# Batch 0's opening rearranged: compact transposes, f32 warm-ups, a later read of the state, and first loads on two queues

## The chip, the cores and the metric

The kernel runs on one core of one Trainium2 chip. The metric is device time in microseconds (us), as a median of executions. The profile is one execution taken by the hardware profiler; its span is some 1.8 us shorter than the timed value (147.9 against 149.7 us). In its lines PE is TensorE, PEld its weight loads, DVE is VectorE, ACT is ScalarE, POOL is GpSimd, SPq and ACTq are the instruction queues of SyncE and ScalarE where they issue transfers, and L85 is a line of the kernel's source.

## The reference

Attention between tokens and a small recurrent state, in both directions, and then a layer of two experts with an elementwise maximum:

```python
# x (8, 8, 512, 64), state (8, 8, 32, 64), f32
a  = softmax(scale * x @ state.T);  xread = a @ state      # 512 rows per batch
a2 = softmax(scale * state @ x.T);  sread = a2 @ x         # 32 rows per batch: "the state's read"
X  = concatenate([xread, sread], axis=2)                   # as 4352 rows of 512
out = maximum(X @ w1, X @ w2) @ w_out                      # 512 -> 1024 -> 512
```

The kernel uses maximum(h1, h2) = h2 + relu(h1 - h2). So it needs W1 - W2 for the first layer, and adds W2 @ W_out, which it computes once, to the second. It also multiplies the small state into W1 - W2 first, so that each token needs only its row of `a` and the product.

## The kernel before

All loads go through SyncE's queue. The first ones, in order: batch 0's state (64 KB, in pieces of 256 B), batch 0's x in two halves of 512 KB (even and odd heads, in pieces of 1 KB), then W2 and W_out (pieces of 2 KB), W1, and batch 1's x.

```python
def load_x(b, parts=1):
    xf_t[b] = xio.tile([128, H, NC * D], F32, ...)
    for g in range(parts):
        nc.sync.dma_start(out=xf_t[b][:, g::parts, :], in_=x[b, g::parts].rearrange("h (p c) d -> p h (c d)", c=NC))

def load_states(bs):
    nc.sync.dma_start(out=s_f[...], in_=state[bs].rearrange("b (q h) n d -> (h n) (b q) d", q=2))
...
load_states(first)
load_x(0, 2)
for ch in range(2):
    load_w(w2f, moe_w2, ch); load_wo(2 * ch); load_wo(2 * ch + 1)
load_w(w1f, moe_w1, 0, 2)          # first half of W1, in two pieces
load_w(w1f, moe_w1, 1)
load_x(1)
```

The work up to the first matmul on W1, in program order (each engine runs its own part in this order). `warm_up(n)` issues n matmuls on zeros that are meant to keep the array at its full rate; the letters A, V, P name ScalarE, VectorE, GpSimd.

```python
warm_up(6)
cast_states("V", first)
states(first)                  # two transposes of the state
warm_up(9)
cast_x(0, (("A", even heads), ("V", even), ("P", odd), ("V", odd)))  # f32 -> bf16, with a ones column
u_xt(0, 0, "V")                # transposes of the even half of x: 16 of 128x64
warm_up(2)
u_xt(0, 1, "A")                # the odd half
u_exp(0, 0); warm_up(2); u_exp(0, 1); warm_up(3)      # scores, exp
w_cast(w2b, w2f, 0, "PA")
u_norm(0, 0, nc.vector)        # row sums "es", reciprocals "er", multiply: a = e * er
u_norm(0, 1, nc.vector)
w_t(0, 0, "A"); w_t(0, 1, "A") # transposes of W2
u_sr(0)                        # the state's read: 32 matmuls
wo_cast(0, "P"); wo_cast(1, "P"); warm_up(1)
...w_wo(0, i)                  # W2 @ W_out, first quarter of the sum
u_at(0, "V")                   # transposes of a
w_cast(w2b, w2f, 1)
...w_wo(1, i)
w_t(1, 0, "V"); w_t(1, 1, "A")
negate_states()                # V: sneg = -state
wo_cast(2, "P"); wo_cast(3, "P")
u_srt(0); warm_up(2)           # one transpose of the state's read
...w_wo(2, i), casts of W1's first half on P, A, V, A, ...w_wo(3, i)
u_sw(0, 0)                     # state @ W1 - state @ W2: the first matmuls on W1
...
w_sub(0); w_sub(1)             # P: W1 - W2, first half
l1(0, {}, range(0, 4))         # layer 1 of batch 0
```

The softmax here doesn't subtract the row's maximum and nothing guards it: scores larger than these inputs give would overflow.

Of the kernel before, what the change touches and what calls it, by code (L numbers as in the profile page):

```python
# [8 lines left out]
F32 = mybir.dt.float32  # L9
BF16 = mybir.dt.bfloat16  # L10
# [5 lines left out]
def kernel(  # L16
# [42 lines left out]
    def copy(eng, o, i):  # L59
        if eng == "A":  # L60
            nc.scalar.copy(o, i)  # L61
        elif eng == "V":
            nc.vector.tensor_copy(o, i)  # L63
        else:
            nc.gpsimd.tensor_copy(o, i)  # L65
# [8 lines left out]

    xf_t = {}

    def load_x(b, parts=1):
        xf_t[b] = xio.tile([128, H, NC * D], F32, tag="xf", name="xf")
        for g in range(parts):
            nc.sync.dma_start(out=xf_t[b][:, g::parts, :], in_=x[b, g::parts].rearrange("h (p c) d -> p h (c d)", c=NC))  # L80

    s_f = stage.tile([128, 2 * B, D], F32)

    def load_states(bs):
        nc.sync.dma_start(out=s_f[:, 2 * bs.start:2 * bs.stop],  # L85
                          in_=state[bs].rearrange("b (q h) n d -> (h n) (b q) d", q=2))

    first, second, rest = slice(0, 1), slice(1, 3), slice(3, 8)
# [11 lines left out]
        nc.sync.dma_start(out=wof[:, 2 * q:2 * q + 2],  # L100
                          in_=moe_w_out.rearrange("(k p) n -> p k n", p=128)[:, 2 * q:2 * q + 2])

    load_states(first)
    load_x(0, 2)
    for ch in range(2):
        load_w(w2f, moe_w2, ch)
        load_wo(2 * ch)
# [5 lines left out]
    load_x(2)  # L113

    ident = consts.tile([128, 128], BF16)
    warm = consts.tile([128, 512], BF16)
    nc.gpsimd.memset(warm, 0.0)  # L117
    make_identity(nc, ident)
    sbd = consts.tile([128, B, H, 2, Ns], BF16)
# [8 lines left out]
    def warm_up(n):  # L128
        p = bank()
        for k in range(n):  # L130
            nc.tensor.matmul(p, warm[:, 0:128], warm, start=(k == 0), stop=(k == n - 1))  # L131


    s_bf = stage.tile([128, 2 * B, 2, D], BF16)
# [16 lines left out]
    def states(bs):  # L151
        p = bank(BF16)
        n = bs.stop - bs.start
        for q in range(2 * n):
            nc.tensor.transpose(p[:, q * 128:(q + 1) * 128], s_bf[:, 2 * bs.start + q].rearrange("p u d -> p (u d)"), ident)
        for g in range(2):
            copy("V", sbd[64 * g:64 * g + 64, bs, :, g, :],
                 p[64 * g:64 * g + 64, 0:256 * n].rearrange("p (b h n) -> p b h n", b=n, h=H))
# [16 lines left out]
    def cast_x(b, parts=(("P", slice(0, 8)),)):  # L175
        new_x(b)
        xp = st[b]["xp"] = xio.tile([128, H, NC, 66], BF16, tag="xp", name="xp")
        nc.gpsimd.memset(xp[:, :, :, 64:65], 1.0)
        for e, hs in parts:
            copy(e, xp[:, hs, :, 0:64], xf_t[b][:, hs].rearrange("p h (c d) -> p h c d", c=NC))  # L180

    def compact_x(b, g, eng="A"):
        new_x(b)
        if g == 0:
            st[b]["xc"] = at.tile([128, H, NC * D], BF16, tag="xc", name="xc")
        copy(eng, st[b]["xc"][:, 4 * g:4 * g + 4], xf_t[b][:, 4 * g:4 * g + 4])


    def d_xt(b):
# [2 lines left out]
    def u_xt(b, g, eng):  # L192
        d = st[b]
        p = bank(BF16)
        for i in range(4):
            for c in range(NC):
                k = 2 * i + c // 2
                nc.tensor.transpose(p[64 * (c % 2):64 * (c % 2) + 64, k * 128:(k + 1) * 128], d["xp"][:, 2 * i + g, c, 0:64], ident)
        copy(eng, d["xt"].rearrange("p (i g u) t -> p g i (u t)", g=2, u=2)[:, g], p.rearrange("p (i w) -> p i w", i=4))

    def u_sc(b, g, mul=nc.gpsimd):
# [28 lines left out]
    def u_sr(b):  # L230

        d = st[b]
        d["sr"] = at.tile([128, 2, D], BF16, tag="sr", name="sr")
        d["rr"] = at.tile([128, 2], F32, tag="rr", name="rr")
        p = bank()
        for g in range(2):
            for c in range(NC):
                for i in range(4):
                    nc.tensor.matmul(p[32 * i:32 * i + 32, g * 65:g * 65 + 65], d["e"][:, g, i, c, :],  # L239
                                     d["xp"][:, 2 * i + g, c, 0:65],  # L240
                                     start=(c == 0 and g == 0), stop=(c == NC - 1 and g == 1))
        pv = p[:, 0:130].rearrange("p (g u) -> p g u", g=2)
        nc.vector.reciprocal(d["rr"], p[:, 64:130:65])
        nc.vector.tensor_mul(d["sr"], pv[:, :, 0:64], d["rr"].unsqueeze(2).to_broadcast([128, 2, D]))
# [16 lines left out]
    def u_srt(b):  # L261
        p = bank(BF16)
        nc.tensor.transpose(p[:, 0:128], st[b]["sr"].rearrange("p g d -> p (g d)"), ident)
        copy("A", sread_t[:, :, b * Ns:(b + 1) * Ns], p[:, 0:128].rearrange("p (i n) -> p i n", i=4))
        del st[b]
# [36 lines left out]
    def l1(b, fill, fs=range(NF), engs=None):  # L302
        if fs[0] == 0:
            R[b] = big.tile([128, NF, NC * 128], BF16, tag="r", name="r")
        for f in fs:
            p = bank()
            for g in range(2):
                nc.tensor.matmul(p, SW[b][:, g, f * 128:(f + 1) * 128], AT[b][:, g, :], start=(g == 0), stop=(g == 1))  # L308
            relu(R[b][:, f, :], p, engs and engs[f - fs[0]])
            run(*fill.get(f, ()))  # L310
# [10 lines left out]
    def l2_add(b, c, fs):  # L321
        for f in fs:
            nc.tensor.matmul(OB[b][1 + c], R[b][:, f, c * 128:(c + 1) * 128], wo[:, f, :], start=False, stop=(f == NF - 1))  # L323
# [94 lines left out]
    def fillers(b):  # L418
        fill = {}

        def put(slot, *units):
            fill.setdefault(slot, []).extend(units)

        n = b + 1
        if n < B:
            put(7, lambda: u_sc(n, 0), lambda: u_sc(n, 1))
            put(8, lambda: u_sr(n))
        if n + 1 < B:
            put(8, lambda: compact_x(n + 1, 0), lambda: compact_x(n + 1, 1))
        if n < B:  # L430
            put(9, lambda: d_at(n))
            put(10, lambda: u_sw(n, 0, 1, 2))
        if n + 1 < B:
            put(10, lambda: d_xt(n + 1))
        if n < B:
            put(11, lambda: u_srt(n))
        return fill

    for b in range(B):
        SW[b] = swt[:, b % 2]  # L440
    warm_up(6)
    cast_states("V", first)
    states(first)
    warm_up(9)
    cast_x(0, (("A", slice(0, 4, 2)), ("V", slice(4, 8, 2)), ("P", slice(1, 4, 2)), ("V", slice(5, 8, 2))))
    u_xt(0, 0, "V")
    warm_up(2)
    u_xt(0, 1, "A")
    u_exp(0, 0)
    warm_up(2)  # L450
    u_exp(0, 1)
    warm_up(3)
    w_cast(w2b, w2f, 0, "PA")
    u_norm(0, 0, nc.vector)
    u_norm(0, 1, nc.vector)
    w_t(0, 0, "A")
    w_t(0, 1, "A")
    u_sr(0)
    wo_cast(0, "P")
    wo_cast(1, "P")  # L460
    warm_up(1)
    for i in range(4):
        w_wo(0, i)
    u_at(0, "V")
# [5 lines left out]
    negate_states()  # L470
    wo_cast(2, "P")
    wo_cast(3, "P")
    u_srt(0)
    warm_up(2)
    for i in range(4):
        w_wo(2, i)
    for e, i in (("P", slice(0, 1)), ("A", slice(1, 2)), ("V", slice(2, 3)), ("A", slice(3, 4))):
# [9 lines left out]
    l1(0, {}, range(0, 4))  # L487
    w_sub(2, nc.vector)
    w_sub(3, nc.vector)
    compact_x(1, 0)  # L490
    compact_x(1, 1)
    d_xt(1)
    load_states(rest)
    cast_x(1, (("A", slice(0, 4)), ("A", slice(4, 8))))
    cast_states("P", second)
    compact_x(2, 0, "P")
    compact_x(2, 1, "P")
    d_xt(2)
    load_x(3)
    for c in range(NC):  # L500
# [1 line left out]
    l2_add(0, 0, range(0, 4))  # L502
    l2_add(0, 1, range(0, 4))
    states(second)
    l2_add(0, 2, range(0, 4))
    u_sw(0, 1)
    l2_add(0, 3, range(0, 4))
    l1(0, {}, range(4, 8))
    u_sw(1, 0)
    u_exp(1, 0)  # L510
    u_exp(1, 1)
# [61 lines left out]
```

## Time and profile before

Before the change: 149.76 us (149.66 to 149.92, 4 runs). The moments, from the timelines of single engines:

| moment (us from the span's start) | before |
|---|---|
| state landed, VectorE casts it | 2.91 |
| even / odd half of x landed, cast | 5.13 / 6.67 |
| transposes of x begin, even / odd half | 6.13 / 7.62 |
| first row sums "es" | 9.84 |
| TensorE waits for W_out's third quarter, then goes on | 0.72, then 18.71 |
| W1's first half landed | 21.64 |
| first matmul on W1 | 22.25 |
| layer 1 of batch 0 | 23.92 |
| layer 1 of batch 1 | 40.01 |

A line of a timeline gives start, duration, engine, source line, operation, output and inputs, shapes and count; a bracket at its end is idle time of that engine just before, and what ended it.

### The profile page before, as it was taken

To read this page: it belongs to the slowest core of one execution; us is meant where nothing else is said; L and a number is where in the kernel's file an instruction comes from. 1 tells how busy PE (TensorE), PEld (TensorE's weight loads), DVE (VectorE), ACT (ScalarE), POOL (GpSimd) and SP (SyncE) were. 2 spreads that over 40 slices of the span, in tenths; PEclk is the share of its full clock that TensorE was granted. 3 is DMA by queue.
4 is the path that set the end of the run, shared out by engine and by line. 5 is a ranking of instruction groups with operands and counts; after the bars stand their busy time and mean duration, and the time that the engine had idled before them with its cause. 6 is when DMAs were issued, how large, how long until landed. Compare 5 with 4: busy or idle time off the path is not lost.

```text
span 147.9 us, 3003 instructions
## 1 busy us (share of the span) xinstructions
PE 139.4 (94%) x1228; PEld 67.4 (46%) x1249; DVE 81.7 (55%) x150; ACT 75.7 (51%) x127; POOL 44.2 (30%) x48
## 2 busy tenths in 40 slices
PE   6979899999999999999999999999999999999991
PEld 2445433434454345434443454454445434764460
DVE  5448728758887187545836581668067635721130
ACT  3175538577576268446834691477167036521011
POOL 3144269551967310640072037004100500000000
PEclk9999999999999999999999999999999999999999
DMA  4999999879999939793979497760556031502423
GB/s 75 379 387 387 387 385 340 269 138 231 262 230 307 303 68 297 273 195 118 285 226 178 177 280 188 139 284 2 106 111 284 0 75 58 226 0 70 141 89 131
DMA packets 37982, 29.89 MB, mean 202 GB/s; under 512 B 24912, under 2 KB 33360, under 8 KB 37072
## 3 DMA queue, kind: packets, MB, share of 16 engines
q1 hardware_dynamic: 37824, 29.56, 69.6%
q8 instruction: 10, 0.16, 0.4%
q10 hardware_dynamic: 144, 0.13, 0.3%
q14 instruction: 4, 0.03, 0.1%
HBM read 15.20 MB, written 8.91 MB: 163 GB/s over the span
## 4 chain that ended last, share of the span: by engine, by line
PE 74%; DMA 14%; SPq 7%; ACT 2%; issue 1%
PE acc L323 34%; PE ps L308 16%; DMA xf<-in_x_dram 11%; PE acc L319 8%; SPq L97 4%; DMA xt<-xc 3%; PE ps L280 3%; PE ps L216 2%; PE ps L367 2%; PE acc L377 2%; PE ps L239 2%; SPq L100 2%; PE acc L357 1%; ACT xc L61 1%; PE acc L375 1%
## 5 line engine op out<-in xcount | busy, mean ns | idle before, releaser
L323 PE MATMUL acc<-wo,r 128*128 128x512 bf16 x238 | 58.3, 379 | 0.5
L323 PEld LDWEIGHTS <-r 128*128 128x128 bf16 x248 | 23.9, 98 | 28.3 <-issue 0.2
L298 DVE TENSOR_SCALAR r<-ps 128x512 bf16<-128x512 f32 x32 | 22.1, 692 | 13.6 <-PE ps L308 13.6
L226 POOL TENSOR_TENSOR a<-e,er 128x512 bf16<-128x512 bf16 x14 | 14.4, 1049 | 50.5 <-ACT e L219 29.6
L308 PE MATMUL ps<-aT,swt 128*128 128x512 bf16 x127 | 29.1, 379 | 0.3 <-DVE swt L63 0.2
L63 DVE COPY ob<-acc 128x512 f32<-128x512 f32 (+1 forms) x17 | 11.0, 655 | 30.2 <-PE acc L323 29.8
L61 ACT COPY ob<-acc 128x512 f32<-128x512 f32 (+1 forms) x16 | 9.2, 573 | 28.9 <-PE acc L323 13.1
L296 ACT ACTIVATE r<-ps 128x512 bf16<-128x512 f32 x32 | 19.2, 600 | 5.8 <-PE ps L308 5.2
L308 PEld LDWEIGHTS <-swt 128*128 128x128 bf16 x128 | 12.0, 98 | 15.0 <-DVE swt L63 0.8
L319 PE MATMUL acc<-swt,aT 128*128 128x512 bf16 x56 | 16.7, 380 | 0.9 <-issue 0.8
L61 ACT CAST swt<-ps 128x512 bf16<-128x512 f32 x18 | 10.0, 588 | 13.0 <-PE ps L280 13.0
L65 POOL CAST xp<-xf 128x2048 bf16<-128x2048 f32 (+1 forms) x7 | 12.2, 1745 | 11.0 <-DMA xf<-in_x_dram 11.0
L61 ACT CAST xc<-xf 128x1024 bf16<-128x1024 f32 x12 | 11.9, 1051 | 1.6 <-DMA xf<-in_x_dram 1.6
L223 DVE TENSOR_REDUCE es<-e 128x16 f32<-128x512 bf16 x16 | 10.6, 660 | 3.6 <-ACT e L219 3.6
L63 DVE CAST swt<-ps 128x512 bf16<-128x512 f32 x18 | 11.6, 678 | 1.1 <-PE ps L280 1.1
L219 ACT ACTIVATE e<-ps 128x512 bf16<-128x512 f32 x16 | 8.8, 596 | 0.8
L131 PE MATMUL ps<-warm 128*128 128x512 bf16 x24 | 7.7, 444 | 1.3 <-POOL warm L117 1.3
L412 PE MATMUL acc<-wo,w2t 128*128 128x512 bf16 x30 | 7.3, 379 | 0.8 <-POOL wo L65 0.7
L319 PEld LDWEIGHTS <-aT 128*128 128x128 bf16 x62 | 4.7, 98 | 5.9 <-issue 2.5
L280 PE MATMUL ps<-wcat,sbd 64*32 64x512 bf16 x136 | 6.2, 383 | 0.1
L216 PEld LDWEIGHTS <-xt 128*128 128x128 bf16 x128 | 4.8, 98 | 2.8 <-ACT xt L61 0.8
L216 PE MATMUL ps<-sbd,xt 128*128 128x64 bf16 x128 | 5.3, 193 | 0.7 <-ACT xt L61 0.6
(74 smaller groups left out, 118.2 us busy)
## 6 DMA issues: line engine op xcount, KB each, us to landing
xf<-in_x_dram SPq DMA_DIRECT2D x7, 1024.0 KB, 7.6
out_dram<-ob SPq DMA_DIRECT2D x7, 1024.0 KB, 5.0
w2f<-in_moe_w_dram SPq DMA_DIRECT2D x2, 1024.0 KB, 8.9
wof<-in_moe_w_out_dram SPq DMA_DIRECT2D x4, 512.0 KB, 10.8
xf<-in_x_dram SPq DMA_DIRECT2D x2, 512.0 KB, 4.4
w1f<-in_moe_w_dram SPq DMA_DIRECT2D x2, 512.0 KB, 13.5
w1f<-in_moe_w_dram SPq DMA_DIRECT2D x1, 1024.0 KB, 14.4
out_dram<-ob SPq DMA_DIRECT2D x3, 256.0 KB, 2.2
```

Of the source, the lines that this page charges most:

```text
L61: nc.scalar.copy(o, i)
L63: nc.vector.tensor_copy(o, i)
L65: nc.gpsimd.tensor_copy(o, i)
L216: nc.tensor.matmul(p[:, k * 64:k * 64 + 64], d["xt"][:, 4 * i + 2 * g + cp, :], sbd[:, b, 2 * i + g].rearrange("p u n -> p (u n)"), start= ...
L223: nc.vector.tensor_reduce(d["es"][:, g], d["e"][:, g].rearrange("p i c n -> p (i c) n"), axis=mybir.AxisListType.X, op=ALU.add)
L226: mul.tensor_mul(d["a"][:, g].rearrange("p c i n -> p i c n"), d["e"][:, g], d["er"][:, g].rearrange("p (i c) -> p i c", i=4).unsqueeze(3) ...
L280: nc.tensor.matmul(pg[g][32 * i:32 * i + 32, :], sneg[gs, i, :] if k else sbd[gs, b, 2 * i + g, g, :], w[gs, i, ch * 512:(ch + 1) * 512], ...
L296: nc.scalar.activation(out=o, in_=p, func=ACTF.Relu)
L298: nc.vector.tensor_scalar(o, p, scalar1=0.0, scalar2=None, op0=ALU.max)
L308: nc.tensor.matmul(p, SW[b][:, g, f * 128:(f + 1) * 128], AT[b][:, g, :], start=(g == 0), stop=(g == 1))
L319: nc.tensor.matmul(OB[b][1 + c], AT[b][:, g, c * 128:(c + 1) * 128], SW[b][:, g, FF:WC], start=(g == 0), stop=False)
L323: nc.tensor.matmul(OB[b][1 + c], R[b][:, f, c * 128:(c + 1) * 128], wo[:, f, :], start=False, stop=(f == NF - 1))
```

## The change

Its intent is to reach W1 with fewer TensorE instructions: compact bf16 x needs 16 transposes of 128x128 instead of 32 of 128x64; 8 warm-ups in f32 replace 25 in bf16; the state's read moves behind the start of layer 1, and with it the cast with the ones column becomes one GpSimd instruction later on. Beside that, the first loads are spread over two queues.

```diff
-    def load_x(b, parts=1):
+    def load_x(b, engs=(nc.sync,)):
...
-    load_states(first)
-    load_x(0, 2)
+    load_states(first, nc.scalar)
+    load_x(0, (nc.sync, nc.scalar))
...
-    warm = consts.tile([128, 512], BF16)
+    warm = consts.tile([128, 256], F32)
...
-            for c in range(NC):
-                k = 2 * i + c // 2
-                nc.tensor.transpose(p[64 * (c % 2):64 * (c % 2) + 64, k * 128:(k + 1) * 128], d["xp"][:, 2 * i + g, c, 0:64], ident)
+            for cp in range(2):
+                k = 2 * i + cp
+                nc.tensor.transpose(p[:, k * 128:(k + 1) * 128], d["xc"][:, 2 * i + g, cp * 128:(cp + 1) * 128], ident)
...
-    warm_up(6)
+    warm_up(2)
     cast_states("V", first)
     states(first)
-    warm_up(9)
-    cast_x(0, (...))
+    warm_up(5)
+    compact_x(0, (...))             # the same four engines and parts
     u_xt(0, 0, "V")
-    warm_up(2)
     u_xt(0, 1, "A")
     u_exp(0, 0)
-    warm_up(2)
     u_exp(0, 1)
-    warm_up(3)
+    warm_up(1)
...
-    u_sr(0)
     wo_cast(0, "P")
     wo_cast(1, "P")
-    warm_up(1)
+    cast_x(0)                       # one GpSimd cast of 128x2048
...
-    u_srt(0)
-    warm_up(2)
...
     states(second)
+    u_sr(0)                         # behind layer 1's first half
...
     l1(0, {}, range(4, 8))
+    u_srt(0)
```

More of the change, by code (lines that the diff above doesn't have):

```diff
@@ L75, with load_states @@
     xf_t = {}
-    def load_x(b, parts=1):
+    def load_x(b, engs=(nc.sync,)):
         xf_t[b] = xio.tile([128, H, NC * D], F32, tag="xf", name="xf")
-        for g in range(parts):
-            nc.sync.dma_start(out=xf_t[b][:, g::parts, :], in_=x[b, g::parts].rearrange("h (p c) d -> p h (c d)", c=NC))
+        parts = len(engs)
+        for g, eng in enumerate(engs):
+            eng.dma_start(out=xf_t[b][:, g::parts, :], in_=x[b, g::parts].rearrange("h (p c) d -> p h (c d)", c=NC))
     s_f = stage.tile([128, 2 * B, D], F32)
-    def load_states(bs):
-        nc.sync.dma_start(out=s_f[:, 2 * bs.start:2 * bs.stop],
+    def load_states(bs, eng=nc.sync):
+        eng.dma_start(out=s_f[:, 2 * bs.start:2 * bs.stop],
                           in_=state[bs].rearrange("b (q h) n d -> (h n) (b q) d", q=2))
@@ L130, in warm_up @@
         for k in range(n):
-            nc.tensor.matmul(p, warm[:, 0:128], warm, start=(k == 0), stop=(k == n - 1))
+            nc.tensor.matmul(p[:, 0:256], warm[:, 0:128], warm, start=(k == 0), stop=(k == n - 1))
     s_bf = stage.tile([128, 2 * B, 2, D], BF16)
@@ L180, in cast_x, with compact_x @@
             copy(e, xp[:, hs, :, 0:64], xf_t[b][:, hs].rearrange("p h (c d) -> p h c d", c=NC))
-    def compact_x(b, g, eng="A"):
+    def compact_x(b, parts=(("A", slice(0, 4)), ("A", slice(4, 8)))):
         new_x(b)
-        if g == 0:
-            st[b]["xc"] = at.tile([128, H, NC * D], BF16, tag="xc", name="xc")
-        copy(eng, st[b]["xc"][:, 4 * g:4 * g + 4], xf_t[b][:, 4 * g:4 * g + 4])
+        xc = st[b]["xc"] = at.tile([128, H, NC * D], BF16, tag="xc", name="xc")
+        for e, hs in parts:
+            copy(e, xc[:, hs], xf_t[b][:, hs])
     def d_xt(b):
@@ L428, in fillers @@
         if n + 1 < B:
-            put(8, lambda: compact_x(n + 1, 0), lambda: compact_x(n + 1, 1))
+            put(8, lambda: compact_x(n + 1))
         if n < B:
@@ L440 @@
         SW[b] = swt[:, b % 2]
-    warm_up(6)
+    warm_up(2)
     cast_states("V", first)
     states(first)
-    warm_up(9)
-    cast_x(0, (("A", slice(0, 4, 2)), ("V", slice(4, 8, 2)), ("P", slice(1, 4, 2)), ("V", slice(5, 8, 2))))
+    warm_up(5)
+    compact_x(0, (("A", slice(0, 4, 2)), ("V", slice(4, 8, 2)), ("P", slice(1, 4, 2)), ("V", slice(5, 8, 2))))
     u_xt(0, 0, "V")
-    warm_up(2)
     u_xt(0, 1, "A")
     u_exp(0, 0)
-    warm_up(2)
     u_exp(0, 1)
-    warm_up(3)
+    warm_up(1)
     w_cast(w2b, w2f, 0, "PA")
@@ L489 @@
     w_sub(3, nc.vector)
-    compact_x(1, 0)
-    compact_x(1, 1)
+    compact_x(1)
     d_xt(1)
@@ L495 @@
     cast_states("P", second)
-    compact_x(2, 0, "P")
-    compact_x(2, 1, "P")
+    compact_x(2, (("P", slice(0, 4)), ("P", slice(4, 8))))
     d_xt(2)
```

## The prediction

> **What bounds the kernel now.** I read the page of the kernel before first, then the chain of work that ended last in order of time, then the timeline of single engines over the first 46 us, the waits, and busy time in short windows from the start.
>
> The page, its head, its row of slices and its chain by engine:
>
> ```profile
> span 147.9 us, 3003 instructions
> PE 139.4 (94%) x1228; PEld 67.4 (46%) x1249; DVE 81.7 (55%) x150; ACT 75.7 (51%) x127; POOL 44.2 (30%) x48
> ...
> DMA  4999999879999939793979497760556031502423
> GB/s 75 379 387 387 387 385 340 269 138 231 262 230 307 303 68 297 273 195 118 285 226 178 177 280 188 139 284 2 106 111 284 0 75 58 226 0 70 141 89 131
> ```
>
> TensorE is busy nearly everywhere. But the DMA engines run flat at some 385 GB/s from the second slice to the sixth, 3.7 to 22.2 us, and never again for so long. So there are two stages: up to about 22 us the loads (batch 0's x and state, W2, W_out, first half of W1) may be the limit, after it TensorE. The chain says the same: it goes through one transfer, then through matmuls alone.
>
> ```profile
> 11.39 16.16 DMA xf<-in_x_dram
> 27.55 0.02 issue
> 27.57 1.99 ACT xc L61 x2
> 29.57 0.03 ACT xp L61
> 29.59 4.50 DMA xt<-xc
> 34.10 0.04 issue
> 34.14 0.71 PE ps L216 x16
> ```
>
> The transfer is batch 1's x, queued behind all weights. The changed region ends at 22.25 us, where the first matmuls on W1 start. The timeline of TensorE before it:
>
> ```profile
> 16.44 1.06 PE L401 MATMUL ps<-ident,w2b 128*128 128x128 bf16 x16
> 17.34 0.22 PE L263 MATMUL ps<-ident,sr 128*128 128x128 bf16 x1
> 17.39 0.59 PE L131 MATMUL ps<-warm 128*128 128x512 bf16 x2
> 18.71 3.61 PE L412 MATMUL acc<-wo,w2t 128*128 128x512 bf16 x15 [0.72 <-POOL wo L65]
> 22.25 0.45 PE L280 MATMUL ps<-w1b,sbd 64*32 64x512 bf16 x8
> ```
>
> and of GpSimd, ScalarE and VectorE, the casts that it needs:
>
> ```profile
> 17.61 1.04 POOL L65 CAST wo<-wof 128x1024 bf16<-128x1024 f32 x1 [4.41 <-DMA wof<-in_moe_w_out_dram]
> 21.64 0.62 ACT L61 CAST w1b<-w1f 128x512 bf16<-128x512 f32 x1 [0.74 <-DMA w1f<-in_moe_w_dram]
> 21.64 0.43 DVE L63 CAST w1b<-w1f 128x512 bf16<-128x512 f32 x1 [2.74 <-DMA w1f<-in_moe_w_dram]
> ```
>
> The square bracket is idle time before and what ended it. TensorE was done with the work of this stage at about 17.9 us, stood 0.72 us, and went on when GpSimd had cast the third quarter of W_out, which had waited 4.41 us for its load. From 18.71 sixteen matmuls run back to back to 22.2; W1's last piece lands at 21.64 and its cast ends at 22.26. So two paths meet at 22.25, and both start at a landing. TensorE's own instruction count ahead of W1 is not what sets this moment.
>
> **What the Trainium skill says.** "DMA: Bandwidth & Descriptors", section "Issuing engines are not separate DMA queues": issuing from several engines saves only the sequencer's issue time. The trace has that time: 0.45 us for the state, 0.50 us each for two halves of x, all on one queue before W2's issue at 2.29 us. "TensorE: Matmul & The Clock Gate", Part 1: the array runs at half rate until about 3.4 us of activity and falls back after such a stretch of idleness. The trace agrees on the first: six warm-ups take 2.74 us from 1.31 us, nine later ones 2.14 us. "FP8 and Floating Point Precision", "TensorE Precision Notes": true f32 takes four passes; no f32 matmul is in this trace. "Runtime: NRT & Kernel Launch", "Instruction fetch mechanics": instructions come in blocks of 256 and crossing a block is mostly hidden. TensorE's list of waits up to 60 us holds no wait on a fetch, so I see none to save.
>
> **The change part by part.** Everything before 22.25 counts only if it moves the landings; everything after adds to TensorE's stream.
>
> 1. Transposes. 32 of 128x64 become 16 of 128x128. Sixteen old ones take 0.64 us; eight of the new shape exist already on W2 and take 0.62 us. So half the instructions save 2 x 0.02 = 0.04 us, in a stage with slack: nothing. The halves of x are cast compactly; the copy with a ones column becomes one GpSimd cast of 128x2048, 1.89 us as at 39.61. GpSimd is free from 13.2 to 17.6, so it fits with some 2.5 us to spare.
>
> 2. Warm-ups. 25 bf16 ones of 512 columns become 8 f32 ones of 256. With four passes each is worth 1024 columns, two old ones: 16 old ones' worth, 9 x 0.216 = 1.9 us less (0.216 is 1.73 us / 8 from the chain's rows of eight). This is idle filler. In instructions: 25+2+32+16+32+32+32+8+1 = 180 matmuls before W1 become 8+2+16+16+32+32+8 = 114, each with a weight load: 360 to 228.
>
> 3. State's read moved. 32 matmuls, 0.37 us (chain, 46.26), and one transpose, 0.06 us (54.09), go from the slack before 17.9 us to behind W1, into a full stream. From 22.25 to 34.10 TensorE is busy 11.35 of 11.85 us. That is 0.43 us added at the end. The transpose also takes one of four "ps" banks. At 33.61 the next pair of matmuls took the banks of the ReLUs that had ended at 33.0 and 33.54; shifted by one they wait for the one ending at 33.88, and the scores after them for that ending at 34.41. I put 0.2 us of waits on it, an estimate. Sum +0.63 us.
>
> 4. First loads. State and half of x go to ScalarE's queue, so x is issued at 0.74 instead of 1.25, and W2 at about 1.25 instead of 2.29. The windows of the start:
>
> ```profile
> 2.00:2.25 0.25, 0.25 (x2) 0.11 (x1) 0.25 (x1) 0.01 (x1) 0.00 (x0) 1.00 0.74 165
> 2.25:2.50 0.25, 0.25 (x2) 0.04 (x1) 0.25 (x1) 0.00 (x0) 0.00 (x0) 1.00 1.14 76
> 2.75:3.00 0.25, 0.25 (x3) 0.00 (x1) 0.25 (x2) 0.00 (x0) 0.00 (x0) 1.00 0.31 29
> 3.25:3.50 0.25, 0.25 (x2) 0.08 (x1) 0.00 (x0) 0.00 (x0) 0.00 (x0) 1.00 0.93 324
> ```
>
> The last column is GB/s. The state comes in near 2 us and full rate starts at 3.25, although x was issued from 1.25 on. At least the 0.51 us of issue is won; if x also stood behind the state's small pieces in the one queue, it could flow 0.7 us after its issue ends, as the state did (1.19 to about 1.9), and 1.2 us is won. I take 0.8. The bytes up to W1's first half are unchanged, and the engines are saturated to 22 us, so every later landing moves by the same: W_out's quarter 17.6 to 16.8, W1 21.64 to 20.8. TensorE must be free by then: its work before 17.9 shrinks by 0.37 + 0.06 and by three warm-ups of 0.216 in the busy stretch from 12 us on, 1.1 us in all, and its inputs come 0.8 earlier. It will be.
>
> Sum: -0.8 + 0.63 = -0.2; 149.7 - 0.2 = 149.5; as the slack could absorb some of the bank waits, I say 149.4 us.
>
> **The rivals.** (a) The transfer start does not move: state and x share sixteen engines, and the low rate from 2.25 to 3.25 is a first-access delay that any load pays. For it: the DMA share is 1.14 at 76 GB/s, so the engines were occupied and slow, not empty. Then only the added 0.4 to 0.6 us remains: 150.2. (b) TensorE becomes the limit before W1 by its clock: with the warm-ups between the stages gone it is busy perhaps 1.9 of 4 us from 6 to 10 us. If it falls to half rate, the sixteen matmuls and eight transposes from 12.5 to 16.4 take up to 3.4 us more at worst, and about 1.8 us of slack (0.72 + 1.1) take most of it: up to 151. Against it: no gap is near 3.4 us. (c) The long GpSimd cast blocks VectorE: the normalising multiply took 1.45 us beside a GpSimd cast at 10.85 and 0.69 us at 13.22. If the second one meets the 1.89 us cast, batch 0's transposes slip by about 1.5 us; the same slack takes it, so 149.4 to 150. (d) A wait on instruction fetch that no record shows ends ahead of W1: then a gain up to the 0.72 us, but the landing holds it there anyway. (e) The start moves the full 1.2 us and the moved work falls in holes: 149.7 - 1.2 + 0.2 = 148.7.
>
> **Range and chances.** Between (e) and (a) with some of (b): 148.7 to 150.5. A change over 2% is 3.0 us. Faster by that would need the 125 us after W1 to shrink, where work is only added; slower would need the half clock well beyond W1. Within 2%: 0.97; faster 0.01; slower 0.02.
>
> **What would show it.** In the changed kernel's trace: full DMA rate from about 2.4 us rather than 3.25; W1's last cast at about 20.8; first matmul on W1 at about 21.4; TensorE still standing for W_out's cast before that; u_sr's 32 matmuls and a short wait on a ReLU or a bank between 28 and 35 us; the length from the first W1 matmul to the end some 0.6 us longer than the 125.6 us of before. Wrong I am if the first W1 matmul waits for TensorE's own earlier work, if transposes or matmuls after 8 us last twice as long, or if the length after W1 changes by more than 1 us, for which I see no cause.

## The result and the profile after

The changed kernel took **153.47 us** (153.32 to 154.02, 4 runs) against 149.76 us: ratio 1.0253, 95% interval 1.0225 to 1.0281, so it is slower by 2.5%. (A ratio is the mean time of one kernel's fast runs over that of the other's fast runs of the same rounds, so it is not quite the ratio of the medians quoted.) The prediction of 149.4 us, with 148.7 to 150.5 as its range, was wrong.

The page of the kernel after, with the lines that answer to those of before:

```profile
span 151.6 us, 2977 instructions
PE 142.2 (94%) x1224; PEld 70.0 (46%) x1224; DVE 86.2 (57%) x150; ACT 75.7 (50%) x127; POOL 46.5 (31%) x49
...
DMA  4999999549969993987798397943376030602423
GB/s 110 382 378 388 387 381 333 187 82 180 212 212 312 306 193 138 307 189 133 240 311 150 64 305 260 189 152 143 68 139 274 7 69 0 281 0 58 129 95 135
```

Nothing is alarming here. The loads do start earlier: the first slice carries 110 GB/s instead of 75. Over the first 5 us, the same stretch in both, it is 180 GB/s instead of 154, so 0.13 MB more, worth some 0.34 us at 385 GB/s. The bandwidth is as good as before. What changed is who got it. Once all of x was in, hardly anything of the lead was left for the weights: the second half of W2 landed at 14.62 us instead of 14.73. The chain of work that ended last, after, in order of time (start, duration, what):

```profile
1.24 8.81 DMA xf<-in_x_dram
...
10.11 0.87 POOL xc L65
...
14.24 2.12 DVE a L227
...
18.43 1.73 PE acc L413 x8
...
21.38 1.14 DVE sneg L68
22.54 2.48 DVE sneg L68
```

Before, the chain went through the load of *batch 1's* x. Now it goes through that of half of *batch 0's* x, issued at 1.24 us and underway for 8.81 us; then through a multiply that lasts 2.12 us and two halves of the negation of the state, 3.6 us together. VectorE is on the chain for 7% of the span; before, it did not appear there. TensorE's timeline after:

```profile
9.63 1.06 PE L199 MATMUL ps<-ident,xc 128*128 128x128 bf16 x8
...
21.44 3.63 PE L413 MATMUL acc<-wo,w2t 128*128 128x512 bf16 x16 [0.34 <-DVE w2t L63]
25.00 0.93 PE L281 MATMUL ps<-w1b,sbd 64*32 64x512 bf16 x8
...
27.33 1.90 PE L309 MATMUL ps<-aT,swt 128*128 128x512 bf16 x8 [0.21 <-DVE swt L63]
```

The transposes of x begin at 9.63 instead of 6.13 us. The sixteen matmuls that before waited 0.72 us for GpSimd's cast of W_out now start at 21.44 instead of 18.71 and wait for TensorE's own earlier work (a VectorE copy of its transposes). Side by side:

| moment | before | after | later by |
|---|---|---|---|
| state cast | 2.91 | 4.72 | 1.81 |
| even / odd half of x cast | 5.13 / 6.67 | 5.00 / 10.08 | -0.13 / 3.41 |
| first row sums | 9.84 | 13.23 | 3.39 |
| W_out's third quarter multiplied | 18.71 | 21.44 | 2.73 |
| W1's first half landed | 21.64 | 20.12 | -1.52 |
| first matmul on W1 | 22.25 | 25.00 | 2.75 |
| layer 1 of batch 0 | 23.92 | 27.33 | 3.41 |
| layer 1 of batch 1 | 40.01 | 43.68 | 3.67 |
| end of the span | 147.9 | 151.6 | 3.7 |

So the 3.7 us can be followed. 3.4 us come in with x; some 0.7 us of that vanish in the slack before W_out; 0.66 us come back between the first matmul on W1 and layer 1, beside the long negation; 0.26 us come with the state's read; the rest of the kernel repeats. And W1 itself landed 1.5 us *earlier*, which helped nobody: of this only 0.1 us are the earlier start of the loads (see W2's second half), and the rest is looked into below.

Why did x come late? The transfers of the first 30 us, before, and then after (size, median us from issue to landing):

```profile
xf<-in_x_dram SPq DMA_DIRECT2D x2, 512.0 KB, 4.4
...
s_f<-in_state_dram SPq DMA_DIRECT2D x1, 64.0 KB, 2.0
```

```profile
xf<-in_x_dram SPq DMA_DIRECT2D x1, 512.0 KB, 4.2
xf<-in_x_dram ACTq DMA_DIRECT2D x1, 512.0 KB, 8.8
...
s_f<-in_state_dram ACTq DMA_DIRECT2D x1, 64.0 KB, 4.0
```

What was issued on ScalarE's queue took twice as long; what stayed on SyncE's did not. The transfers in progress from 7 to 8 us after the start, by queue (q1 is SyncE's, q10 ScalarE's; packets, MB, share of 16 engines):

```profile
q1 hardware_dynamic: 129, 0.25, 69.2%
q10 hardware_dynamic: 126, 0.13, 38.3%
```

Both queues moved the same *number* of packets, but W2's on q1 are 2 KB and x's on q10 are 1 KB, so x got a third of the bytes. This is what "DMA: Bandwidth & Descriptors" of the Trainium skill states in its section "Queues, rings and completion order": each engine goes round between the queues that have work, packet by packet. (A packet of that page holds several descriptors. That it is the same as a packet of the profile is not shown; what is shown is that the profile's numbers are equal.) The prediction had cited the section on issuing engines of the same page and not this one. Before, x stood ahead of W2 in one queue and got all the bandwidth until it was through.

### The profile page after: what moved, and what is told of

The parts are those of the page before. It is cut to its first block, busy times and chain, and to the rows that moved or that the text cites. A ratio compares the mean times of both kernels' runs of the same rounds, so it can differ in the third digit from the quotient of the medians.

```text
span 151.6 us, 2977 instructions
## 1 busy us (share of the span) xinstructions
PE 142.2 (94%) x1224; PEld 70.0 (46%) x1224; DVE 86.2 (57%) x150; ACT 75.7 (50%) x127; POOL 46.5 (31%) x49
## 4 chain that ended last, share of the span: by engine, by line
PE 82%; DVE 7%; DMA 6%; ACT 1%; POOL 1%; issue 0%; ACTq 0%
PE acc L324 36%; PE ps L309 18%; PE acc L320 10%; DMA xf<-in_x_dram 6%; PE ps L281 3%; DVE sneg L68 2%; PE ps L368 2%; PE acc L378 2%; PE ps L217 2%; PE ps L240 2%; DVE a L227 2%; PE acc L358 1%; PE acc L413 1%; PE acc L376 1%; DVE es L224 1%; PE acc L281 1%
## 5 line engine op out<-in xcount | busy, mean ns | idle before, releaser
L324 PE MATMUL acc<-wo,r 128*128 128x512 bf16 x248 | 59.0, 379 | 0.0
L320 PE MATMUL acc<-swt,aT 128*128 128x512 bf16 x62 | 18.1, 381 | 0.0
L65 POOL CAST xp<-xf 128x2048 bf16<-128x2048 f32 x7 | 13.2, 1889 | 9.4 <-DMA xf<-in_x_dram 9.4
L61 ACT CAST xc<-xf 128x1024 bf16<-128x1024 f32 (+1 forms) x13 | 12.6, 1017 | 1.9 <-DMA xf<-in_x_dram 1.9
L132 PE MATMUL ps<-warm 128*128 128x256 f32 x16 | 7.3, 624 | 1.1 <-POOL warm L118 1.1
L65 POOL CAST xc<-xf 128x1024 bf16<-128x1024 f32 (+1 forms) x3 | 4.3, 1439 | 10.8 <-DMA xf<-in_x_dram 10.8
L281 PE MATMUL ps<-wcat,sbd 64*32 64x512 bf16 x136 | 6.8, 383 | 0.2 <-DVE wcat L63 0.2
```

The source lines that it names most:

```text
L61: nc.scalar.copy(o, i)
L65: nc.gpsimd.tensor_copy(o, i)
L281: nc.tensor.matmul(pg[g][32 * i:32 * i + 32, :], sneg[gs, i, :] if k else sbd[gs, b, 2 * i + g, g, :], w[gs, i, ch * 512:(ch + 1) * 512], ...
L320: nc.tensor.matmul(OB[b][1 + c], AT[b][:, g, c * 128:(c + 1) * 128], SW[b][:, g, FF:WC], start=(g == 0), stop=False)
L324: nc.tensor.matmul(OB[b][1 + c], R[b][:, f, c * 128:(c + 1) * 128], wo[:, f, :], start=False, stop=(f == NF - 1))
```

## The experiments

My theory after the result was that the loads alone make the loss: the state and half of x stand one behind the other in a queue that shares packet by packet with coarse weight loads. The rivals were the warm-ups (f32, and a cold array, which means one at half rate: the ten rows of warm-ups after the state ran at 0.44 us each instead of some 0.22), ScalarE's queue as such, and a change in W1's path. Each run had the kernel before beside it on the same chip. Ratios are against those runs, with 95% intervals.

### Loads or warm-ups?

`a_one_queue` is the changed kernel with the loads back on one queue; `a_bf16_warm` with bf16 warm-ups of about the same length instead of f32 ones; `a_both_undone` with both; `b_two_queues` is the kernel before with nothing but the two queues.

```diff
 a_one_queue                                  # changed kernel
-    load_states(first, nc.scalar)
-    load_x(0, (nc.sync, nc.scalar))
+    load_states(first)
+    load_x(0, (nc.sync, nc.sync))
 a_bf16_warm                                  # changed kernel
-    warm = consts.tile([128, 256], F32)
+    warm = consts.tile([128, 512], BF16)     # and warm_up(4), (10), (2) for (2), (5), (1)
 b_two_queues                                 # kernel before
-    load_states(first)
-    load_x(0, 2)
+    load_states(first, nc.scalar)
+    load_x(0, (nc.sync, nc.scalar))
```

> The changed kernel with state and both halves of batch 0's x issued from the sync queue again; the f32 warm-ups stay. Theory Q (the second half of x landed at 10.1 us instead of 6.7 because the ScalarE queue's share of the transfer engines is small beside W2 and W_out) expects that half cast at 6.7 us, first W1 matmul at about 22.5 us, time 149.8 to 150.5. Theory W (TensorE was held to 9.63 us by ten f32 rows of 0.437 us) expects TensorE still held: rows of 0.437 us from about 3.3 us to 7.7 us, transposes 1.5 us late, time 151 to 152. Theory M (moved state's read, transposes and the long GpSimd cast cost the time) expects 153.4.

> The changed kernel with two bf16 warm-ups of 512 columns for each f32 one of 256 (4, 10 and 2), the two queues stay. Q expects the second half of x still at about 10.1 us and 153.0 to 153.6 us. W expects TensorE free at about 7.5 us and 150.0 us. M expects 153.4.

> The changed kernel with one queue and bf16 warm-ups: what is left of the change are the 16 transposes, the later cast with the ones column, the fewer warm-ups and the state's read behind W1. Q and W expect 150.0 us (0.3 us over before for the state's read). M expects over 152 us.

> The kernel before with only the first loads on two queues. Q expects the second half of x at about 10 us and 152.3 to 153.3 us, most of the loss from this part alone. W expects a small gain, 149.3 us. M expects 149.3 to 149.7 us.

| run | us | ratio | odd half of x cast | layer 1 of batch 0 |
|---|---|---|---|---|
| a_one_queue | 150.73 | 1.0053 (1.0024 to 1.0083) | 7.34 | 24.91 |
| a_bf16_warm | 153.53 | 1.0234 (1.0203 to 1.0264) | 10.13 | 27.34 |
| a_both_undone | 150.82 | 1.0058 (1.0028 to 1.0089) | 6.86 | 24.43 |
| b_two_queues | 154.16 | 1.0264 (1.0221 to 1.0306) | 10.26 | 28.53 |

One queue takes nearly all of the loss away and two queues alone make all of it. (The profiled run of `a_one_queue` is its slowest, 151.20 us, which makes its two moments some 0.5 us late. `b_two_queues` is even slower than the 152.3 to 153.3 expected: there VectorE's cast of W1 met a long GpSimd instruction, took 2.68 us instead of 0.43, and TensorE waited 1.22 us for it.) The type of the warm-ups does nothing: with bf16 the changed kernel is as slow, and the ten rows after the state take 4.47 us instead of 4.58. `a_both_undone` leaves 0.6%, where 150.0 us was expected; the next parts look into it. In `b_two_queues` the half of x on ScalarE's queue is as slow as in the changed kernel:

```profile
xf<-in_x_dram ACTq DMA_DIRECT2D x1, 512.0 KB, 9.0
```

### Which property of the two queues?

If ScalarE's queue as such were slow, x would be late there in any place. `b_even_act` is the kernel before with the even half of x alone, first, on ScalarE's queue. `a_state_sync` is the changed kernel with one word undone: only the state goes back to SyncE, so that the half of x is first in its queue and runs beside the other half, of equal pieces. `a_w2_1k` leaves both on ScalarE's queue but cuts W2's first MB into 1 KB pieces, so that equal turns become equal bytes.

```diff
 b_even_act                                   # kernel before
-    load_states(first)
-    load_x(0, 2)
+    load_states(first)
+    load_x(0, (nc.scalar, nc.sync))
 a_state_sync                                 # changed kernel
-    load_states(first, nc.scalar)
+    load_states(first)
 a_w2_1k                                      # changed kernel
-        load_w(w2f, moe_w2, ch)
+        ...for ch == 0: two loads of 256 columns each instead of one of 512
```

> The kernel before, with the even half of x first and alone on the ScalarE queue, state and the odd half on the sync queue. Theory P (transfer engines take one packet from each queue in turn, so a queue of 1 KB pieces gets a third beside one of 2 KB pieces, and a later place behind the state's small pieces costs more) expects both halves landed by about 6.2 us, every later landing 0.3 to 0.6 us earlier, and 149.2 to 149.7 us. Theory S (the ScalarE queue is slow in itself) expects the half on it at 9 us or later and over 152 us.

> The changed kernel with W2's first 1 MB loaded in two transfers of 256 columns, 1 KB pieces instead of 2 KB. P expects equal bytes for the two queues while both run: the half of x on the ScalarE queue cast at about 8.7 us instead of 10.1, time about 152.4 us. S expects 10.1 us and 153.4 us still.

> The changed kernel with one word undone: the state on the sync queue, first; half of x alone on the ScalarE queue. Theory P (a later place behind small pieces and beside 2 KB pieces makes it late) expects that half landed by 6.7 us and 150.4 to 150.9 us. Rival: any split on two queues costs, half of x stays later than 8 us and the time over 152.

`b_even_act` took 149.69 us (0.9991, 0.9976 to 1.0005): the half on ScalarE's queue landed 4.3 us after its issue, so the queue is not slow. `a_state_sync` took **150.22 us** (1.0023, 1.0004 to 1.0041): one word takes the loss from 2.5% to 0.2%. Its transfers:

```profile
xf<-in_x_dram ACTq DMA_DIRECT2D x1, 512.0 KB, 4.3
xf<-in_x_dram SPq DMA_DIRECT2D x1, 512.0 KB, 5.2
```

The same half of x in the same queue lands 4.3 us after its issue instead of 8.8, because it no longer stands behind the state: in the changed kernel the state's pieces moved from 3 to 4.25 us and x's only from about 5.2 us on, when the even half was through on the other queue and W2 was flowing there.

`a_w2_1k` tests the sharing itself. Its transfers from 7 to 8 us:

```profile
q1 hardware_dynamic: 185, 0.19, 59.5%
q10 hardware_dynamic: 163, 0.16, 50.2%
```

Now bytes are nearly equal, and the odd half was cast at 8.76 instead of 10.08, as expected. So equal pieces take back 1.3 of the 3.4 us. The other 2.1 are mostly what any sharing leaves: the odd half's pieces begin to move between 4.5 and 5.1 us in this run, in the changed kernel and in the kernel before, but only in the last with nothing beside them. But the time, 153.79 us (1.0262, 1.0249 to 1.0276), missed the expectation by 1.4. The trace says why: the ten cold rows of warm-ups held TensorE until 9.61 whatever x did; of the 1.3 us, 0.67 were left at the row sums and 0.16 at W_out; and the negation took 4.13 us, so that layer 1 began at 27.59. The mechanism of the delay is shown, and also that x was not the only thing standing in that place: the array, still at half rate, was nearly as late. That the 1.9 us of waiting for the state had made it cold is not shown. These are the ten rows of the changed kernel, and of `a_one_queue`, where TensorE did not wait for the state at all:

```profile
5.26 4.58 PE L132 MATMUL ps<-warm 128*128 128x256 f32 x10
```

```profile
3.39 4.36 PE L132 MATMUL ps<-warm 128*128 128x256 f32 x10
```

In `a_neg_early`, after a wait of 2.0 us, the same ten rows took 3.69 us. When the full rate comes differs from run to run.

### What the other parts cost

`b_state_late` is the kernel before with only the state's read moved. `au_cast_act` is `a_both_undone` with the cast of the ones column on ScalarE instead of GpSimd. `a_neg_early` is the changed kernel with the negation right behind the state's transposes. `a_no_block` is that with the cast on ScalarE too.

```diff
 b_state_late                                 # kernel before
-    u_sr(0)                                  # after w_t(0, 1)
-    u_srt(0)                                 # after the casts of W_out
     states(second)
+    u_sr(0)
...
     l1(0, {}, range(4, 8))
+    u_srt(0)
 au_cast_act                                  # a_both_undone
-    cast_x(0)
+    cast_x(0, (("A", slice(0, 4)), ("A", slice(4, 8))))
 a_neg_early                                  # changed kernel
     states(first)
+    negate_states()
...
-    negate_states()                          # behind the second transposes of W2
```

> The kernel before with only the state's read and its transpose moved behind W1. Expected 0.3 to 0.6 us more than before (0.43 us of work in a full TensorE stream, perhaps 0.2 us of bank waits), 150.1 us beside 149.7. Rival: it falls into holes of the stream and nothing changes.

> The changed kernel with one queue and bf16 warm-ups (150.8 us), and the cast with the ones column on ScalarE instead of GpSimd. If the GpSimd cast blocked VectorE's second normalising multiply (2.42 us instead of 0.69) and through it delayed W1's first matmul by 0.7 us, that multiply is back at 0.7 us and the time falls by 0.5 to 0.7 us to about 150.2. Rival: ScalarE's later W2 cast delays TensorE as much, and it stays at 150.8.

> The changed kernel with VectorE's negation of the state moved ahead of GpSimd's W1-W2 subtraction, right after the state's transposes. If the blocked negation (3.7 us for two, 0.7 to 1.2 elsewhere) is what puts 0.66 us between W1's first matmul and the first layer-1 matmul, layer 1 starts at about 26.7 instead of 27.3 us and the time is 152.8 us. Rival: VectorE's W1 cast, next in its order, is blocked in its place and it stays at 153.4.

> As the run with the early negation, and the cast with the ones column on ScalarE instead of GpSimd; x's half still late. If blocking of VectorE by GpSimd is what adds to the late half, the normalising multiplies are at 0.7 us again, layer 1 starts at about 26.1 us and the time is about 152.2 us; what is left over the version before is then the late half alone. Rival: no change from 152.8 to 153.4.

`b_state_late`: 150.56 us, 1.0045 (1.0029 to 1.0061, 6 runs), so the moved read costs some 0.7 us there. In the profiled run (150.84 us) layer 1 of batch 0 starts at 24.00 and that of batch 1 at 41.13, 17.13 us apart instead of 16.09. Of these 1.04 us, 0.47 are this wait:

```profile
35.34 0.64 PE L216 MATMUL ps<-sbd,xt 128*128 128x64 bf16 x16 [0.47 <-DMA xt<-xc]
```

It waits for the transposed x of batch 1, a transfer that does not get earlier when TensorE's work is shifted. In the changed kernel everything else is so late that this wait is gone, and the same move costs only 0.26 us (3.41 to 3.67 in the table).

Then the two engines that share a way into memory. In `a_both_undone`, the second multiply on VectorE, GpSimd's cast, and TensorE's transposes of `a`, from three timelines:

```profile
13.45 2.42 DVE L227 TENSOR_TENSOR a<-e,er 128x512 bf16<-128x512 bf16 x1
```

```profile
13.44 1.88 POOL L65 CAST xp<-xf 128x2048 bf16<-128x2048 f32 x1
```

```profile
15.93 0.40 PE L258 MATMUL ps<-ident,a 128*128 128x128 bf16 x4 [1.28 <-DVE a L227]
```

The multiply that takes 0.69 us alone starts 0.01 us after the cast and ends 0.55 us after it. "SBUF — State Buffer" of the Trainium skill, section "SBUF: two separate sides", calls what the two engines share "an exclusive lock", held for the whole instruction, and counts among those concerned VectorE operations with two inputs in this memory. The trace agrees. On ScalarE the cast does not slow the multiply: in `au_cast_act` the multiply is back at 0.69 us and W_out's third quarter starts at 17.81. But the total was 150.66 us (1.0057, 1.0044 to 1.0069), no better, since W1 landed at 21.62 and TensorE waited for it there. The expectation of 150.2 missed that second wait.

The negation was the costlier case. In the changed kernel, on VectorE and on GpSimd:

```profile
21.30 3.72 DVE L68 TENSOR_SCALAR sneg<-sbd 64x128 bf16<-64x128 bf16 x2
```

```profile
20.12 4.67 POOL L387 TENSOR_TENSOR wcat<-w1f,w2f 128x1024 bf16<-128x1024 f32 x2 [0.69 <-DMA w1f<-in_moe_w_dram]
```

Two small negations, 1.21 us together before, end within 0.25 us of GpSimd's subtraction W1 - W2. That started at 20.12 as soon as W1 had landed; before, it started at 21.69, when the negation was long done. So the early W1 started the very instruction that blocked VectorE, and the late x had put the negation beside it (in `a_state_sync`, with W1 as early and x on time, the negations ran at 18.96 and took 0.66 us). In `a_neg_early` the two negations took 0.41 us at 6.24, layer 1 began at 26.60 instead of 27.33 (26.7 was expected), and the time was 152.67 us (1.0189, 1.0167 to 1.0211): some 0.7 us of the loss is this. `a_no_block` freed the multiply too, and won nothing clear (152.49 us, 1.0177, 1.0157 to 1.0197; layer 1 at 26.72). In its profiled run (152.78 us, granted clock 0.989) TensorE's transposes of W2 took 1.92 us for sixteen, where two times 0.62 is usual, as at half rate, so that it came to `a` only at 18.14. The other three runs, listed at clock 1.0, took 152.37 to 152.51, some 0.2 us under `a_neg_early`; why they gain no more is not shown. Its expectation of 152.2 was not met.

### Why W1 landed earlier, and whether it can be used

The loads end nearly as before, yet W1's first half landed 1.5 us earlier. The transfers from 15 to 16 us of the kernel before hold one packet that the program did not ask for:

```profile
q8 instruction: 1, 0.02, 7.0%
```

It is a block of some 16 KB of instructions (0.15 MB for 9 on the page after), and 7.0% of 16 engines for 1 us is one engine for 1.1 us. In the kernel after, this packet comes from 21 to 22 us, when W1 is in. My theory F, formed here: fewer TensorE instructions ahead of W1 put off the fetch of TensorE's next block, and a fetch holds one of the 16 transfer engines, so that the weight load spread over them ends later. The rival R: W1 is earlier for another reason, and a kernel that keeps the early W1 without the late x would win. The landings, seen where GpSimd's or VectorE's wait for them ends:

| run | instruction packet | W_out's third quarter | W1, first piece | W1, second piece |
|---|---|---|---|---|
| before | 15.1 | 17.61 | 20.31 | 21.64 |
| after | 21.7 | 16.02 | by 18.82 | 20.12 |
| a_tiny40 | 16.8 | 16.29 | 20.05 | 21.44 |
| s_cast_act | 17.8 | 15.90 | 18.60 | 21.05 |
| s_cast_act_few (slow) | 22.7 | 15.96 | 18.68 | 20.05 |

The first three runs below were made to separate F from R. `a_tiny40` adds 40 tiny matmuls to the changed kernel in the idle time before the state; F wants the packet earlier and W1 late. `s_cast_act` is `a_state_sync` with the cast on ScalarE. `s_cast_act_few` cuts its 8 warm-ups to 2, so that few instructions are left. `b_even_act_w5` is `b_even_act` with 4 instead of 9 warm-ups before x.

```diff
 a_tiny40                                     # changed kernel
     warm_up(2)
+    p = bank()
+    for k in range(40):
+        nc.tensor.matmul(p[:, 0:16], ident, ident[:, 0:16], start=(k == 0), stop=(k == 39))
     cast_states("V", first)
 s_cast_act                                   # a_state_sync
-    cast_x(0)
+    cast_x(0, (("A", slice(0, 4)), ("A", slice(4, 8))))
 s_cast_act_few                               # s_cast_act
-    warm_up(2) ... warm_up(5) ... warm_up(1)
+    warm_up(1) ... warm_up(1)
```

> The changed kernel with 40 matmuls of 16 columns added in TensorE's idle time before the state's transposes, 80 instructions more ahead of W1. Theory F (one 16 KB packet of TensorE instructions holds one transfer engine for about 1.1 us, and W1's share on that engine lands 1.3 to 1.6 us later when the packet goes ahead of it) expects the packet at about 17 us instead of 21.7, and GpSimd's wait for W1's first half to end at 21.3 to 21.7 instead of 20.1 us; the time stays within 0.5 us of 153.4, since W1's landing is not what this kernel waits for. Rival R (the landing differs for another reason) expects 20.1 us still.

> The changed kernel with the state on the sync queue (150.2 us) and the cast with the ones column on ScalarE, so that GpSimd does not block VectorE's second normalising multiply. TensorE's last eighth of W2 times W_out then ends 1.2 us earlier, at about 21.4 us. F expects the packet at about 18 us, so before W1's landing, which goes back to 21.3 us or later; layer 1 starts at 23.6 us and the time stays at about 150.0 us. R expects W1 at 20.1 us and 149.2 us.

> As the last, with two f32 warm-ups instead of eight (in the trace each makes two weight loads and two matmuls, so 24 instructions fewer). F expects the packet at about 20.7 us, after W1's first half, which lands at 20.1 us; TensorE reaches W1 at about 21.4 us, layer 1 starts at about 23.0 us, time 149.0 to 149.4 us, faster than both kernels. R expects no difference from the run before it. Risk: the array stays at half rate longer and the transposes of x are late.

> The kernel before with the even half of x first on the ScalarE queue (149.7 us, where TensorE was held by nine half-rate warm-ups until 7.4 us) and four warm-ups in place of those nine. Expected: x's transposes at about 6 us, W1's first matmul at its landing, about 21.9 us, and 149.2 to 149.5 us. Rival: the array stays at half rate longer and nothing is won, 149.7 us or more.

`a_tiny40`: the packet came at 16.8 and W1 landed at 21.44, as F expects. The time was 154.79 us (1.0364, 1.0321 to 1.0406), 1.3 more than the changed kernel, which was not expected: the subtraction began later, blocked the negation for longer (4.84 us), and the matmuls on W1 waited 1.26 us for VectorE's cast. I did not separate the parts of that.

`s_cast_act`: 150.02 us (1.0012, 0.9995 to 1.0029), which F gave as 150.0 and R as 149.2. The packet came at 17.8 (F: about 18), between the landings of W_out's third quarter, which is early, and of W1's second piece, which is 2.45 us behind the first instead of 1.3 (at 21.05; F had 21.3 or later). Layer 1 of batch 0 began at 23.33, 0.6 earlier than before the change, but that of batch 1 at 40.40 instead of 40.01: the state's read, and a wait of 0.41 us for batch 1's transposed x, took it back.

`s_cast_act_few`: the packet moved to 22.7 (F: about 20.7) and W1 to 20.05, as F expects. But F's 149.0 to 149.4 us was missed: of six runs four, the profiled one among them, count as slow, being over 1.5% above the fastest (153.3 to 154.9 us), and only two as fast (150.50 and 150.87; 1.0054, 1.0031 to 1.0077). In the profiled one TensorE runs at half rate until about 17 us, although its mean granted clock is listed as 0.998:

```profile
7.12 1.89 PE L199 MATMUL ps<-ident,xc 128*128 128x128 bf16 x16 [2.28 <-ACT xc L61]
...
13.26 3.60 PE L413 MATMUL acc<-wo,w2t 128*128 128x512 bf16 x8
```

They take 1.06 and 1.95 us in `s_cast_act`. This is the prediction's rival (b), which did not come up in `s_cast_act` with its 8 warm-ups. It is a slow run and is compared with nothing here for its total. `b_even_act_w5` took 149.85 us (1.0001, 0.9973 to 1.0029); x's transposes and W1's first matmul came at 5.90 and 21.98 us, as expected, but 149.2 to 149.5 us was not met.

So F's order of packet and landing is met in each run made for it, though not its times. By the landings in the packed traces, in all seventeen kernels the first landing after the *end* of the packet is 1.0 to 1.6 us late; the four landings that fall within the packet's 1.1 us are on time. `a_state_sync` shows both: a packet at 19.4, W1's first half on time at 20.05, and W1's second half at 24.08, 4.0 us later, where 2.7 to 2.9 us pass when no packet comes between.

But fewer instructions alone did not bring W1 forward. With them and one queue the packet came at 20.2 (`a_one_queue`) and 19.7 us (`a_both_undone`), and W1's second piece landed at 22.41 and 21.86. With the late x and all the instructions of the kernel before (`b_two_queues`) they came at 18.6 and 21.49. Only where TensorE was both shorter of instructions and late, as in the changed kernel, did the fetch come after W1's first half; its early landing there is in part a consequence of the delay. No variant is shown to beat the kernel before; `b_even_act` and `b_even_act_w5` equal it.

## Why the prediction was wrong

**Step 4, the first loads: wrong, and the cause.** "At least the 0.51 us of issue is won" did not hold: by bytes the start of the loads gained some 0.34 us, not 0.8, and W2's second half landed 0.1 us earlier. "The bytes up to W1's first half are unchanged [...], so every later landing moves by the same" is the step that failed. It took the two queues for one stream that starts earlier, and every landing to move alike. With two, the turns of the queues decide what lands first: the state landed 1.8 us later and half of x 3.4 us later. The section of the Trainium skill that the prediction did cite says that issuing from several engines saves only issue time; read as a statement on order, it misled. Shown by `b_two_queues` (alone it makes the loss), by `a_state_sync` (one word undone takes the loss from 2.5% to 0.2%) and, for the sharing, by `a_w2_1k` and the packet counts.

**What the 3.4 us became.** The prediction said that TensorE "must be free by then: [...] It will be". It was not, because "its inputs come 0.8 earlier" was false for x: it reached W_out's third quarter 2.7 us later, with some 0.7 us absorbed by the slack that the prediction had seen. Its own test, "Wrong I am if the first W1 matmul waits for TensorE's own earlier work", came true.

**Rival (c), the blocked VectorE: right mechanism, wrong victim.** The multiply was blocked (2.12 us in the changed kernel, 2.42 with one queue), and most of that was hidden: TensorE waited 0.16 us for it in the changed kernel. What cost was the negation, some 0.7 us (`a_neg_early`), which the prediction did not list, since it did not ask what the earlier W1 would start on GpSimd.

**Step 3, the state's read: right in sign and kind.** 0.63 us was predicted; 0.26 us came in the changed kernel and 0.7 us where it was moved alone (`b_state_late`). The wait for batch 1's transposed x in the latter was not foreseen.

**Step 1, the transposes, and step 2, the warm-ups: no gain in time, as predicted.** The f32 warm-ups behave as two bf16 ones each (`a_bf16_warm`). But the prediction took only their number of columns into account, not where they stand: they come after the state, which landed 1.8 us later, and at half rate they held TensorE nearly as long as x did (`a_w2_1k`). The clock, rival (b), was not the cause in the changed kernel, whose chain goes through x's landing and not through the warm-ups.

**Rival (d), the fetch of instructions: dismissed on the wrong view.** The prediction looked for a wait of TensorE. The fetch showed in the transfers instead, as 1.0 to 1.6 us on the first landing after its end. W1's landing moved by 1.5 us where 0.8 was predicted: 0.1 us by the loads, the rest because the fetch came later, for a reason that the prediction had counted and then set aside (360 instructions became 228 by its count, 244 in the trace, where each f32 warm-up is two matmuls and two weight loads), and because TensorE was late. That the sign was right is luck. Nothing waited for W1 in the changed kernel, so it was no gain.

**Left open.** Why x's packets began only at about 5.2 us although the state's were through by 4.3; which instruction number exactly calls for the block; why a packet some 0.7 us ahead of a landing delays it in two kernels with one queue and spares it in others; the parts of `a_tiny40`'s extra 1.3 us; when the full rate of the array comes; and why `a_no_block` was not faster.

## What to carry to other kernels

Before a load is moved to a second queue, write down what stands ahead of it there and what runs beside it: small pieces that share turns with coarse ones get the smaller part of the bandwidth, and what is needed first should finish before the coarse loads begin. When a landing moves earlier, ask which instructions it starts and whom they block, above all long GpSimd work beside small VectorE work on the path. A saving off the path, such as fewer TensorE instructions, can act through something else, such as the fetch of its own instructions; look for it in the transfers and not in the engine's waits, and check that something still waits for what it brings forward.

## What the Trainium skill lacked or had wrong

- "DMA: Bandwidth & Descriptors": the section "Issuing engines are not separate DMA queues" says that issuing from several engines saves only issue time (and that the transfers interleave). Here it also decided who lands first: half of x took 8.8 us from issue to landing, where the halves took 4.4 in the median before. The section "Queues, rings and completion order" gives turns by packet, but lacks the consequence, that queues with pieces of 2 KB and 1 KB share the bytes two to one (129 and 126 packets, 0.25 and 0.13 MB in one us), and that equal pieces bring equal bytes (0.19 and 0.16 MB).
- "Runtime: NRT & Kernel Launch", section "Instruction fetch mechanics": crossing a block is called mostly hidden. Here a block held one transfer engine for 1.1 us while all were full, and the first load to land after it came 1.0 to 1.6 us later than without (W1 at 20.1 or at 21.4 us in the changed kernel without and with 40 tiny matmuls).
- "TensorE: Matmul & The Clock Gate", Part 1: it says that about 3.4 us of sustained activity bring the full rate, but not how dense the activity must be. Rows of warm-ups without a gap fell from 0.43 to 0.22 us each at 4.1 us in the kernel before, at 4.8 in `b_state_late` and at 6.7 in `b_even_act`, all three with the same first warm-ups from 1.31 us on, and in `a_one_queue` not before 7.3 us. In one slow run of `s_cast_act_few` TensorE was busy for some 4.8 of the 6.1 us from 7.12 to 13.26 us and still ran at half rate until about 17 us.
- "SBUF — State Buffer", section "SBUF: two separate sides": nothing wrong; durations would help. A multiply of 128x512 in bf16 went from 0.69 to 2.12 and 2.42 us beside a GpSimd cast, and two negations of 64x128 from 0.41 (`a_neg_early`) to 3.72 us beside a subtraction of 128x1024 in f32, twice.
